# Batch 1's q transposes moved into one group beside its first keys, and half 1's output transposed in two parts

## The chip, the cores and the metric

One core of one Trainium2 chip. The time is the device time of one execution in microseconds (us). Span is what the profiler sees of the same execution; it is 1.7 us less than the time (231.48 against 229.75 us in the profiled run of the kernel before).

## The reference, cut to what matters

```python
# q, k, v: (4 batches, 8 heads, 768 rows, 64); 8 blocks of 96 rows
P = sinkhorn(sort_net)                        # 8 x 8 for each batch and head
k_sorted, v_sorted = P @ blocks(k), P @ blocks(v)
attn = softmax(scale * q_block @ k_sorted_block.T) @ v_sorted_block
x = heads_side_by_side(attn)                  # (3072, 512)
h = x @ w_in                                  # 512 -> 2048
out = (s * relu(h) ** 2 + b) @ w_out          # 2048 -> 512
```

## The kernel before

Rows are done in eight halves of a batch (0 to 7, 384 rows each; half 1 is the second half of batch 0, and batch 1 starts with half 2). `ffn1(t)` makes the hidden layer of half t: for each of eight pairs of hidden blocks, eight products `hps` on TensorE (PE), relu `rt` on ScalarE (ACT), the squaring `gt` on VectorE (DVE). `ffn2(t)` makes the output, `ops`. Between their products PE gets other work from a queue: scores `sc`, attention outputs `pv`, sorted keys `tk`, sorted values `tv`, transposes of q (`tq`) and of attention outputs (`tr`). Each of these fills a PSUM tile that ACT or DVE must copy out. GpSimd (POOL) meanwhile sums the rows of w_out (`csum`) for the bias term.

```python
def t_piece(t, eng, n0=0, nn=HB):      # all head pairs: 16 transposes, one copy by eng
    ...
def t_part(t, hp0, eng, n0, nn):       # head pairs hp0, hp0+1: 8 transposes, one copy
    ...
# the place of the change (cut)
ffn1(0, Queue([seq(SC(1, 2), P(1, 0)), V1(0), seq(SC(1, 3), P(1, 1)), P(1, 2), V1(1), P(1, 3),
               seq(V1(2), V1(3)), lambda: t_piece(1, "v")], 8), 2, 2)
V1(4)()                                # V1: sorted values of batch 1, tv -> ACT copy vn -> DRAM
V1(5)()
q_piece(1, 0, "s")                     # 24 transposes of q, one copy by ACT
...
csums(0, 8)                            # POOL, once half 1's attention output is there
v_read(1, nc.sync)                     # the values come back from DRAM as vs
ffn1(1, ...)
...
ffn2(0, qu)                            # qu: q_piece(1, 2), keys of batch 1, bias product, ...
```

A queue of eight pieces gives one after each pair of hidden blocks. In the traces ACT and DVE start what they are given in the order of the program (ACT in before: rt at 43.37 us, two vn from 43.76, rt at 44.70; DVE gt at 45.26, xt at 45.72).

The softmax here doesn't subtract the row's maximum and nothing guards it: scores larger than these inputs give would overflow.

Of the kernel before, what the change touches and what calls it, by code (L numbers as in the profile page):

```python
# [18 lines left out]
def kernel(  # L19
# [22 lines left out]
    HB = NB // 2  # L42
# [51 lines left out]
    def load_k(rows, prow, n=1):  # L94
        for c0 in range(0, BLK, BLK // n):
            cs = slice(c0, c0 + BLK // n)
            nc.gpsimd.dma_start(out=kb[prow, cs, :], in_=kraw[rows, cs, :])
# [4 lines left out]
    def brows(b):  # L102
        return slice(b * 64, (b + 1) * 64), slice((b % 2) * 64, (b % 2) * 64 + 64)
# [132 lines left out]
    def evac(out, in_, eng):  # L236
        if eng == "v":
            nc.vector.tensor_copy(out=out, in_=in_)  # L238
        else:
            nc.scalar.copy(out=out, in_=in_)  # L240
# [20 lines left out]
    def q_piece(b, hp0, eng):  # L261

        if hp0 == 0:
            QT[b] = qtp.tile([128, NHP, S], BF, tag="qt", name=f"qt{b}")
        ps = psa.tile([128, 2, 1024], BF, tag="a", name="tq")
        for i in range(2):
            for t in range(TQ):
                for e in range(2):
                    nc.tensor.transpose(
                        out=ps[e * 64:(e + 1) * 64, i, t * 128:(t + 1) * 128],  # L270
                        in_=qr[b][:, 2 * (hp0 + i) + e, t, :], identity=ident)
        evac(QT[b][:, hp0:hp0 + 2, :].rearrange("q a (p t) -> q a p t", t=TQ),
             ps[:, :, 0:S].rearrange("q a (t p) -> q a p t", t=TQ), eng)
# [55 lines left out]
    def v_piece1(c0, eng):  # L329

        pr = brows(1)[1]
        ps = psb.tile([128, 8, D], FP, tag="b", name="tv")
        lhsT = pd1[pr].rearrange("p e m i -> p (e m i)")
        hb = BLK // 2
        for hf in range(2):
            nc.tensor.matmul(out=ps[hf * 64:(hf + 1) * 64], lhsT=lhsT,
                             rhs=vb[pr, hf * hb + c0:hf * hb + c0 + 8, :],
                             start=True, stop=True)
        vn = vnp.tile([128, 16, D], BF, tag="vn", name="vn")
        evac(vn[:, 0:8, :], ps, eng)  # L340
        for hf in range(2):
            nc.sync.dma_start(out=dv[1][:, hf * hb + c0:hf * hb + c0 + 8, :],
                              in_=vn[hf * 64:(hf + 1) * 64, 0:8, :])

    def v_piece2(c0, eng):

        ps = psa.tile([128, 16, D], FP, tag="a", name="tv")
        lhsT = pd2.rearrange("p b e m i -> p (b e m i)")
        for i in range(2):
            nc.tensor.matmul(out=ps[:, i * 8:(i + 1) * 8, :], lhsT=lhsT,  # L350
                             rhs=vb[:, c0 + i * 8:c0 + i * 8 + 8, :], start=True, stop=True)
        vn = vnp.tile([128, 16, D], BF, tag="vn", name="vn")
        evac(vn, ps, eng)
        nc.sync.dma_start(out=dv[2][:, c0:c0 + 16, :], in_=vn)
# [81 lines left out]
    def t_piece(t, eng, n0=0, nn=HB):  # L436

        x = X[t]
        if t not in XT:
            XT[t] = xtp.tile([128, NHP, TG], BF, tag="xt", name="xt")  # L440
        if nn < HB:
            t1 = psb.tile([128, 1024], BF, tag="b", name="tr")
            tr = [t1[:, hp * nn * BLK:(hp + 1) * nn * BLK] for hp in range(NHP)]
            src = t1[:, 0:NHP * nn * BLK]
            dst = XT[t][:, :, n0 * BLK:(n0 + nn) * BLK]
            src = src.rearrange("p (a t) -> p a t", a=NHP)
        else:
            t2 = psa.tile([128, 2, 1024], BF, tag="a", name="tr")
            tr = [t2[:, hp // 2, (hp % 2) * TG:(hp % 2 + 1) * TG] for hp in range(NHP)]
            src = t2[:, :, 0:2 * TG]  # L450
            dst = XT[t].rearrange("p (a b) t -> p a (b t)", b=2)
        for hp in range(NHP):
            for n in range(n0, n0 + nn):
                nc.tensor.transpose(out=tr[hp][:, (n - n0) * BLK:(n - n0 + 1) * BLK],
                                    in_=x[:, n, hp * 128:(hp + 1) * 128],
                                    identity=ident[0:BLK, 0:BLK])
        evac(dst, src, eng)

    def t_part(t, hp0, eng, n0, nn):

        if t not in XT:
            XT[t] = xtp.tile([128, NHP, TG], BF, tag="xt", name="xt")
        tr = psa.tile([128, 2, 1024], BF, tag="a", name="tr")
        for i in range(2):
            hp = hp0 + i
            for n in range(n0, n0 + nn):
                nc.tensor.transpose(out=tr[:, 0, (i * nn + n - n0) * BLK:(i * nn + n - n0 + 1) * BLK],
                                    in_=X[t][:, n, hp * 128:(hp + 1) * 128],
                                    identity=ident[0:BLK, 0:BLK])
        evac(XT[t][:, hp0:hp0 + 2, n0 * BLK:(n0 + nn) * BLK],  # L470
             tr[:, 0, 0:2 * nn * BLK].rearrange("p (a t) -> p a t", a=2), eng)
# [16 lines left out]
    def ffn1(t, slot=nothing, n0=0, nn=HB, lead=0):  # L488
        if t not in GT:
            GT[t] = gtp.tile([128, NF, TG], BF, tag="gt", name="gt")  # L490
        gt = GT[t]
        c0, nt = n0 * BLK, nn * BLK
        begun = {}

        def products(f0, hps, part):
            for f in range(2):
                for hp in part:
                    nc.tensor.matmul(out=hps[:, f, 0:nt], lhsT=wi_at(hp, f0 + f),  # L498
                                     rhs=xt_at(t, hp, n0, nn),
                                     start=(hp == 0), stop=(hp == NHP - 1))  # L500

        for f0 in range(0, lead, 2):
            begun[f0] = psa.tile([128, 2, 512], FP, tag="a", name="hps")
            products(f0, begun[f0], range(0, NHP // 2))
        for f0 in range(0, NF, 2):
            if f0 in begun:
                hps = begun[f0]
                products(f0, hps, range(NHP // 2, NHP))
            else:
                hps = psa.tile([128, 2, 512], FP, tag="a", name="hps")  # L510
                products(f0, hps, range(NHP))
            rt = rtp.tile([128, 2, TG], BF, tag="rt", name="rt")
            nc.scalar.activation(out=rt[:, :, 0:nt], in_=hps[:, :, 0:nt], func=AF.Relu)  # L513
            nc.vector.tensor_tensor(out=gt[:, f0:f0 + 2, c0:c0 + nt], in0=rt[:, :, 0:nt],  # L514
                                    in1=rt[:, :, 0:nt], op=ALU.mult)
            slot()
# [59 lines left out]
    def seq(*fs):  # L576
        def run():
            for f in fs:
                f()
        return run  # L580

    def S2(t, hp):
        return lambda: (s_piece(t, hp), s_piece(t, hp + 1))

    def P2(t, hp):
        return lambda: (p_piece(t, hp), p_piece(t, hp + 1))

    def T(t):
        return lambda: x_turn(t)

    def attn(t):
        return [S2(t, 0), nothing, P2(t, 0), S2(t, 2), nothing, P2(t, 2), nothing, T(t)]
# [54 lines left out]
    def P(t, hp, *r):  # L647
        return lambda: p_piece(t, hp, *r)

    def SC(t, hp):  # L650
        return lambda: s_piece(t, hp)

    def V1(i, eng="s"):
        return lambda: v_piece1(i * 8, eng)
# [1 line left out]
    ffn1(0, Queue([P(0, 0, 2, 2), P(0, 1, 2, 2), P(0, 2, 2, 2), P(0, 3, 2, 2),  # L656
                   lambda: q_half(1, "s"), lambda: t_piece(0, "v", 2, 2), SC(1, 0), SC(1, 1)], 8), 0, 2, 2)
    ffn1(0, Queue([seq(SC(1, 2), P(1, 0)), V1(0), seq(SC(1, 3), P(1, 1)), P(1, 2), V1(1), P(1, 3),
                   seq(V1(2), V1(3)), lambda: t_piece(1, "v")], 8), 2, 2)
    V1(4)()  # L660
    V1(5)()
    q_piece(1, 0, "s")


    csum = const.tile([128, d_model], FP)
# [16 lines left out]
    def K(b, c0, nc2, eng):  # L682
        return lambda: k_piece(b, c0, nc2, 1, eng)()

    V2 = [lambda c0=c0: v_piece2(c0, "s") for c0 in range(0, BLK, 16)]
    qu = Queue([nothing, seq(lambda: q_piece(1, 2, "s"), K(1, 0, 16, "v")), nothing,
                seq(K(1, 32, 16, "s"), K(1, 64, 16, "v")), nothing,
                seq(lambda: load_k(*brows(2)), lambda: load_q(2), bias_piece),
                V2[0], S2(2, 0), V2[1], S2(2, 2), V2[2], V2[3], P2(2, 0), V2[4], P2(2, 2), V2[5],
                seq(T(2), S2(3, 0), K(2, 0, 16, "s")), P2(3, 0), nothing,  # L690
# [13 lines left out]
    qu = Queue([S2(4, 0), nothing, nothing, P2(4, 0), nothing, S2(4, 2), nothing, nothing,  # L704
                P2(4, 2), nothing, T(4), nothing, seq(S2(5, 0), K(3, 0, 16, "v")), nothing, nothing,
                P2(5, 0), nothing, seq(S2(5, 2), K(3, 32, 16, "s")), nothing, P2(5, 2),
                K(3, 64, 16, "s"), T(5),
                lambda: q_turn(3), nothing], 24)
# [4 lines left out]
    qu = Queue(attn(6) + attn(7), 24)  # L713
# [36 lines left out]
```

## Time and profile before

| | |
|---|---|
| time, median of 4 runs | 231.46 us (230.92 to 231.69) |
| PE busy | 97% of the span |
| from the pv at 75.62 us to the end | 154.13 us, PE without a gap to its last product, which ends at 226.42 us |

Two more lines of the page of the kernel before, the busy times and the granted PE clock in tenths, one digit for each 5.7 us:

```profile
PE 223.2 (97%) x2034; PEld 136.3 (59%) x2034; DVE 116.0 (50%) x244; ACT 115.7 (50%) x165; POOL 48.1 (21%) x62
...
PEclk9995699999999999999999999999999999999999
```

With PE busy 97%, what is to be won or lost by moving work is idle PE time, a few tenths of a microsecond at a time. The digits 5 and 6 are a stretch at half clock (0.50 granted) near 17 to 27 us.

### The profile page before, as it was taken

The numbers are of one execution on the slowest core, as the hardware profiler recorded it, in microseconds if no ns is written. First come the engines' busy times: TensorE is split into PE (matmuls) and PEld (weight loads), VectorE is DVE, ScalarE is ACT, GpSimd is POOL, SyncE is SP. The second block draws the span as 40 slices with busy tenths as digits, with TensorE's granted clock in tenths as the row PEclk, the third lists the DMA queues.
The fourth block names the chain that finished last, engine by engine and source line by source line (L and its number), as shares of the span: only waits on it lengthen the run. The fifth ranks groups of instructions, "written<-read, shape, count | busy, mean of one in ns | idle before, by whom it ended". The sixth has DMA issues, their size and how long they took to land.

```text
span 229.8 us, 4833 instructions
## 1 busy us (share of the span) xinstructions
PE 223.2 (97%) x2034; PEld 136.3 (59%) x2034; DVE 116.0 (50%) x244; ACT 115.7 (50%) x165; POOL 48.1 (21%) x62
## 2 busy tenths in 40 slices
PE   8979999999999999999999999999999999999994
PEld 5879888765554565665555555655555556654442
DVE  4778666638991554344345843434443634441221
ACT  5268479685358387866621285565322245660000
POOL 7920000299992000008730000000000000000000
PEclk9995699999999999999999999999999999999999
DMA  5899999999399998645999996610115250001212
GB/s 93 137 199 214 223 195 205 227 219 203 70 122 180 314 247 136 126 116 70 133 142 150 183 176 134 76 47 0 49 46 121 87 114 0 3 0 46 86 54 91
DMA packets 46694, 28.90 MB, mean 126 GB/s; under 512 B 35920, under 2 KB 41040, under 8 KB 46160
## 3 DMA queue, kind: packets, MB, share of 16 engines
q0 software_dynamic: 18800, 15.21, 46.5%
q1 hardware_dynamic: 27728, 13.32, 26.8%
q8 instruction: 16, 0.26, 0.5%
q10 hardware_dynamic: 144, 0.07, 0.1%
q14 instruction: 6, 0.05, 0.1%
HBM read 29.63 MB, written 8.65 MB: 167 GB/s over the span
## 4 chain that ended last, share of the span: by engine, by line
PE 80%; DMA 14%; ACT 3%; DVE 1%; issue 0%; SPq 0%
PE hps L498 31%; PE ops L552 30%; DMA dv<-vn 8%; DMA vs<-dv 6%; PE wp L182 6%; PE pv L402 4%; PE sc L375 3%; PE tv L320 2%; PE ops L537 2%; PE tk L294 1%; ACT ks L240 1%; PE tq L254 1%; ACT qt L240 1%; PE tv L350 0%; ACT rt L513 0%
## 5 line engine op out<-in xcount | busy, mean ns | idle before, releaser
L498 PE MATMUL hps<-xt,wi 128*128 128x384 bf16 (+1 forms) x576 | 87.0, 308 | 0.2
L552 PE MATMUL ops<-wo,gt 128*128 128x512 bf16 x368 | 85.8, 379 | 0.0
L498 PEld LDWEIGHTS <-wi 128*128 128x128 bf16 x576 | 53.7, 98 | 30.6 <-issue 1.1
L513 ACT ACTIVATE rt<-hps 128x768 bf16<-128x768 f32 (+1 forms) x72 | 53.1, 740 | 37.0 <-PE hps L498 36.1
L514 DVE TENSOR_TENSOR gt<-rt 128x768 bf16<-128x768 bf16 (+1 forms) x72 | 41.6, 580 | 49.5 <-ACT rt L513 49.3
L552 PEld LDWEIGHTS <-gt 128*128 128x128 bf16 x368 | 34.0, 98 | 37.9 <-issue 0.6
L378 ACT ACTIVATE at<-sc 96x768 bf16<-96x768 f32 x32 | 24.4, 803 | 30.2 <-PE sc L375 30.1
L526 DVE SCALAR_TENSOR_TENSOR ot<-ops,s_bc,bias 128x512 f32<-128x512 f32 x23 | 17.2, 750 | 40.4 <-PE ops L552 40.3
L407 DVE TENSOR_TENSOR x<-pv,rec 96x512 bf16<-96x512 f32 (+1 forms) x36 | 22.6, 628 | 1.3
L240 ACT CAST ks<-tk 64x512 bf16<-64x512 f32 (+1 forms) x32 | 18.6, 582 | 4.2 <-PE tk L294 3.9
L674 POOL TENSOR_TENSOR csum<-csum,wo 128x512 f32<-128x512 f32 x14 | 17.6, 1254 | 1.0
L182 PE MATMUL wp<-zt 128*128 128x256 bf16 x84 | 13.5, 329 | 1.1 <-DVE warm L113 1.1
L402 PEld LDWEIGHTS <-at 96*128 96x128 bf16 (+1 forms) x256 | 12.0, 104 | 4.3 <-DMA vs<-dv 0.8
L238 DVE CAST ks<-tk 64x512 bf16<-64x512 f32 (+1 forms) x20 | 13.1, 654 | 2.1 <-PE tk L294 1.8
L402 PE MATMUL pv<-vs,at 96*128 96x66 bf16 (+1 forms) x256 | 13.0, 199 | 0.4 <-DMA vs<-dv 0.3
L240 ACT CAST vn<-tv 128x512 bf16<-128x512 f32 (+1 forms) x12 | 9.4, 800 | 6.8 <-DMA out_dram<-ot 3.8
L84 POOL DMA_DIRECT2D qr<-in_q_dram x12 | 10.6, 913 | 5.3 <-DMA kb<-in_k_dram 2.9
L375 PEld LDWEIGHTS <-ks 64*96 64x96 bf16 x256 | 8.3, 128 | 5.7 <-issue 4.3
L406 DVE RECIPROCAL rec<-pv 96x8 f32<-96x8 f32 (+1 forms) x36 | 6.9, 193 | 9.1 <-PE pv L402 9.1
L182 PEld LDWEIGHTS <-zt 128*128 128x128 bf16 x84 | 9.5, 117 | 3.2 <-DVE warm L113 1.1
L375 PE MATMUL sc<-qt,ks 64*96 64x96 bf16 x256 | 10.7, 219 | 0.0
L240 ACT COPY qt<-tq 128x768 bf16<-128x768 bf16 (+1 forms) x6 | 5.9, 1014 | 5.0 <-PE tq L254 3.3
(72 smaller groups left out, 97.5 us busy)
## 6 DMA issues: line engine op xcount, KB each, us to landing
out_dram<-ot SPq DMA_DIRECT2D x23, 256.0 KB, 2.8
kb<-in_k_dram POOLq DMA_DIRECT2D x4, 768.0 KB, 11.1
vb<-in_v_dram POOLq DMA_DIRECT2D x4, 768.0 KB, 18.9
wi<-in_moe_w_in_dram POOLq DMA_DIRECT2D x2, 1024.0 KB, 19.6
wo<-in_moe_w_out_dram POOLq DMA_DIRECT2D x2, 1024.0 KB, 32.5
qr<-in_q_dram POOLq DMA_DIRECT2D x12, 128.0 KB, 17.7
dv<-vn SPq DMA_DIRECT2D x6, 256.0 KB, 6.6
vs<-dv POOLq DMA_DIRECT2D x4, 384.0 KB, 13.1
```

What stands on the lines that cost most here:

```text
L182: nc.tensor.matmul(out=wp, lhsT=zt[:, 0:128], rhs=zt, start=True, stop=True)
L240: nc.scalar.copy(out=out, in_=in_)
L375: nc.tensor.matmul(out=sc[:, e, n * BLK:(n + 1) * BLK], lhsT=ks[pr, g0 + n, :], rhs=QT[b][pr, hp, q0:q0 + BLK], start=True, stop=True)
L378: nc.scalar.activation(out=at, in_=sc[:, :, 0:TG], func=AF.Exp, scale=scale)
L402: nc.tensor.matmul(out=pv[e][0:m, (n - n0) * VW:(n - n0 + 1) * VW], lhsT=atf[:, c0:c0 + m], rhs=VS[b][:, gi, :], start=True, stop=True)
L407: nc.vector.tensor_tensor(out=x[:, n0:n0 + nn, hp * 128:(hp + 1) * 128].rearrange("p n (e d) -> p e n d", e=2), in0=pvv[:, :, :, 0:D], in1 ...
L498: nc.tensor.matmul(out=hps[:, f, 0:nt], lhsT=wi_at(hp, f0 + f), rhs=xt_at(t, hp, n0, nn), start=(hp == 0), stop=(hp == NHP - 1))
L513: nc.scalar.activation(out=rt[:, :, 0:nt], in_=hps[:, :, 0:nt], func=AF.Relu)
L514: nc.vector.tensor_tensor(out=gt[:, f0:f0 + 2, c0:c0 + nt], in0=rt[:, :, 0:nt], in1=rt[:, :, 0:nt], op=ALU.mult)
L526: nc.vector.scalar_tensor_tensor(out=ot, in0=ops, scalar=s_bc, in1=bias, op0=ALU.mult, op1=ALU.add)
L552: nc.tensor.matmul(out=ops, lhsT=gt[:, f, m * 128:(m + 1) * 128], rhs=wo_at(f), start=(f == 0), stop=(f == NF - 1))
L674: nc.gpsimd.tensor_tensor(out=csum, in0=csum, in1=wo_at(f), op=ALU.add)
```

## The change

Intent, as the change has it: transposing half 1's output in two parts lets two engines copy it, so that ffn1 of half 1 need not wait for one long copy; the q transposes that filled that wait then stand with the other q transposes and the first keys. The engines of the last copies are balanced anew.

```diff
-                   seq(V1(2), V1(3)), lambda: t_piece(1, "v")], 8), 2, 2)
+                   seq(lambda: t_part(1, 0, "s", 0, HB), V1(2), V1(3)),
+                   lambda: t_part(1, 2, "v", 0, HB)], 8), 2, 2)
     V1(4)()
     V1(5)()
-    q_piece(1, 0, "s")
...
-    qu = Queue([nothing, seq(lambda: q_piece(1, 2, "s"), K(1, 0, 16, "v")), nothing,
-                seq(K(1, 32, 16, "s"), K(1, 64, 16, "v")), nothing,
+    qu = Queue([nothing, seq(lambda: q_piece(1, 0, "s"), lambda: q_piece(1, 2, "v"), K(1, 0, 16, "v")), nothing,
+                seq(K(1, 32, 16, "s"), K(1, 64, 16, "s")), nothing,
```

("s" is ACT, "v" is DVE.)

## The prediction

> **What bounds the kernel now.** I read the page first: TensorE (PE) is busy 97% of the span, VectorE (DVE), ScalarE (ACT) and GpSimd (POOL) 50%, 50% and 21%. PE is the bound, but a share says nothing about a place, so next the chain of waits, in shares and then in order of time. These lines are the shares, and then the stretch up to the first attention output of half 2 (pv at 75.62):
>
> ```profile
> PE 80%; DMA 14%; ACT 3%; DVE 1%; issue 0%; SPq 0%
> ```
>
> ```profile
> 42.82 11.82 DMA dv<-vn
> ...
> 54.66 7.50 DMA dv<-vn
> ...
> 62.69 12.89 DMA vs<-dv
> 75.58 0.05 issue
> 75.62 0.71 PE pv L402 x16
> ```
>
> The chain does not run through PE from 42.8 to 75.6 us. It runs through the sorted values of batch 1: PE makes them (tv), ACT copies them (vn), they go to DRAM and come back as vs, and PE's pv at 75.62 needs them. After 75.62 the chain is PE alone to the end. So whatever the change does between 42.8 and 75.6 us counts only by when PE gets to that pv, and not before 75.58 us. The timeline there:
>
> ```profile
> 74.34 1.03 PE L552 MATMUL ops<-wo,gt 128*128 128x512 bf16 x4
> ...
> 75.62 0.71 PE L402 MATMUL pv<-vs,at 96*128 96x66 bf16 x16 [0.26 <-DMA vs<-dv]
> ```
>
> Four ops matmuls start every 0.216 us (their step in the trace), so PE was free at 74.34 + 4 x 0.216 = 75.20 us and waited to 75.62: 0.42 us. (The 0.26 that the line prints counts from a modelled end.) That is the whole slack on this path. Third, the timeline where the edited code lies, the end of ffn1 of half 0 and the start of ffn1 of half 1:
>
> ```profile
> 43.37 0.49 ACT L513 ACTIVATE rt<-hps 128x384 bf16<-128x384 f32 x1 [0.44 <-PE hps L498]
> ...
> 43.76 1.07 ACT L240 CAST vn<-tv 128x512 bf16<-128x512 f32 x2
> ...
> 44.43 1.14 POOL L672 TENSOR_TENSOR csum<-wo 128x512 f32<-128x512 bf16 x1
> 44.49 0.85 PE L454 MATMUL tr<-ident,x 96*128 96x96 bf16 x16
> 44.70 0.52 ACT L513 ACTIVATE rt<-hps 128x384 bf16<-128x384 f32 x1
> 45.26 0.53 DVE L514 TENSOR_TENSOR gt<-rt 128x384 bf16<-128x384 bf16 x1 [0.83 <-ACT rt L513]
> ...
> 45.65 1.16 POOL L674 TENSOR_TENSOR csum<-csum,wo 128x512 f32<-128x512 f32 x1
> ...
> 45.72 0.94 DVE L238 COPY xt<-tr 128x1536 bf16<-128x1536 bf16 x1
> 45.81 0.70 PEld L269 LDWEIGHTS <-qr 128*64 128x64 bf16 x24 [0.41 <-issue]
> ...
> 46.71 0.11 PEld L498 LDWEIGHTS <-wi 128*128 128x128 bf16 x2 [0.20 <-DVE xt L238]
> ```
>
> Half 1's output is transposed by 16 matmuls at 44.49, copied by one DVE copy at 45.72 that ends at 46.66, and its first product starts at 46.72. In between PE does four tv and the 24 q transposes (tq) from 45.81. A second group like it takes 0.79 us at 59.41 where nothing is waited for; here it holds PE 0.90 us, so PE really waits 0.1 us. The filler fits the copy almost exactly: there is next to nothing to win here.
>
> [...] DVE's squarings gt, and GpSimd's weight sums beside them:
>
> ```profile
> 49.07 0.62 DVE L514 TENSOR_TENSOR gt<-rt 128x768 bf16<-128x768 bf16 x1 [2.41 <-ACT rt L513]
> 50.37 0.75 DVE L514 TENSOR_TENSOR gt<-rt 128x768 bf16<-128x768 bf16 x1 [0.68 <-ACT rt L513]
> ```
>
> ```profile
> 48.12 1.16 POOL L674 TENSOR_TENSOR csum<-csum,wo 128x512 f32<-128x512 f32 x1
> ```
>
> ```profile
> 49.35 1.35 POOL L674 TENSOR_TENSOR csum<-csum,wo 128x512 f32<-128x512 f32 x1
> ```
>
> The sums end at 49.28 and 50.70, the gt at 49.69 and 51.12: each gt ends 0.41 us after a sum, whenever it was ready. For the half-size gt at 45.26 it is 45.79 - 45.57 = 0.22 us. The copies from PSUM (xt) run beside a sum undisturbed: 0.94 us within the sum of 45.65 to 46.81.
> [...] ACT's rt and vn above run one after the other as the program has them.
> [...] In this trace the last ops before a q or key group (59.41, 62.61) holds PE 0.31 us and not 0.216: 0.09 us for a change.
>
> **The change part by part.**
> (1) The q group of heads 0 to 3 leaves the place before ffn1 of half 1 and stands in ffn2 of half 0, in front of the other one and of the first keys. The number of PE instructions stays (4061 rows either way in the built program). Added there: 24 transposes at 28 ns = 0.67 us, without a change of mode of their own. Removed here: 0.90 us, of which 0.79 is work and mode changes.
> (2) Half 1's transposes come in two parts. The first eight stand after the seventh pair of hidden blocks, in front of two tv pairs, and ACT copies them; the other eight stay at the end, and DVE copies them. I lay this out, with durations from the trace (steps from start to start: ACT rt to next 0.39, vn 0.47, a 128x768 copy 0.69 as the earlier qt copies have, a DVE copy of 128x768 0.55 long):
> - PE: products from 42.51 as before, first eight transposes 43.18 to 43.62, two tv pairs to 44.17, last products to 44.84, second eight to 45.28, two tv pairs to about 45.86. The waits of the built program (PSUM banks freed by rt at 43.86 and by x at 44.16) are met in time.
> - ACT: rt 43.37, xt first half 43.76, vn 44.45, vn 44.92, and only then the last rt, at 45.39 to 45.91. Before it ran at 44.70: 0.69 us later, the length of the new copy.
> - DVE: the last gt could start at 45.95. In the old run it got in behind the first sum (end 45.57). Now the second sum, 45.65 to 46.81,[...]: gt ends at 46.81 + 0.22 = 47.02. The second xt copy stands behind it in order: 46.95 to 47.50.
> - PE: ffn1 of half 1 starts at 45.86, does two matmuls (0.33 us: head pairs 0 and 1, in the half that ACT copied) and waits for head pair 2 until about 47.54. It then stands as if it had started at 47.54 - 0.33 = 47.21, and before it was 46.72: **+0.49 us**, in spite of the q group being gone. A hole of 1.35 us opens where 0.1 was.
> (3) The second q copy goes from ACT to DVE, and one key piece (four casts of about 0.6 us) from DVE to ACT. ACT has idle time there (2.1 us before 67.74) and DVE's queue gets lighter by four casts of 0.69 less one copy[...]. The first score piece needs all keys: ACT ends them at about 69.1, PE is there at about 69.7. No cost.
> Sum until that pv: +0.49 + 0.67 = +1.16 us, so PE comes at 75.20 + 1.16 = 76.36. The values land at about 75.6 as before: the chain to them goes through the second vn at 41.73, ahead of the edit, and the last writes of dv wait for the earlier ones to land (issued 54.66), not for vn. So the old 0.42 us wait vanishes, and the rest stays: 76.36 - 75.62 = **+0.74 us**. After it PE has no gap to absorb it. 231.67 + 0.74 = 232.4 us.
>
> **The rivals.**
> (A) The intent comes true: the two halves are copied side by side on two engines and ffn1 of half 1 starts at 45.86, 0.86 us earlier. Then the q group added later takes 0.67 of it, PE is at the pv 0.19 us earlier, and the DMA holds it there anyway: 231.7. For it: two engines, half the copy each. Against: ACT's and DVE's order, both read from the built program.
> (B) The last gt slips in between two sums. Then gt ends at about 46.3, xt at 46.8, ffn1 as if from 46.5: -0.2 + 0.67 = +0.47, less the 0.42: 231.7 to 231.8. For it: the sums leave gaps of 0.08 us. Against: each later gt waited for one to end.
> (C) In ffn2 of half 0 DVE is late: gt there take 1.5 us each and are behind until 61.2, perhaps 62.6 now; then the strided q copy and four casts end at 65.5 to 67, and the bias product, which takes their PSUM bank, is due at 66.5. Up to +0.6: 233.0.
> (D) The dv writes of the two delayed vn (0.7 us) push vs back by as much. To cost, vs would have to land after 76.36; only beyond that it adds. [...] Against: the last issues wait for other writes.
>
> **Range and chances.** (2) as laid out gives 232.4, A and B 231.7, C and D up to 233.0. The three runs before span 0.44 us, so noise is about 0.2. I weigh my layout at six in ten: 232.3 with 231.6 to 233.0. Two per cent are 4.6 us; no rival comes near. [...]
>
> **What would show it.** Right: the last half-size rt at about 45.4, gt ending 0.2 us after a sum, xt ending near 47.5, two hps matmuls and then an idle PE of over 1 us for DVE's xt; 48 tq in a row at about 60 us lasting some 1.45 us; no wait for vs at the pv, which starts at 76.2 to 76.5. Wrong: ffn1 of half 1 going on before 46.7 without a hole, a wait for vs that remains, or a new wait for a PSUM bank at the bias product.

The marked cuts are statements that no trace here shows. That the last gt ends 0.22 us after the second sum is an estimate from the squarings shown (each ends 0.41 us after a sum, the half-size one 0.22). "A change" is one of tile in the trace, from the `128*128` of ops to the `128*64` of tq or the `64*128` of tk. That a sum leaves the copies alone shows in the smaller xt copy, 0.55 us beside a sum (47.06 in after) and 0.55 without one (34.47 in before).

## The result, and the profile after

232.82 us, median of 4 runs (232.77 to 232.94), against 231.46 us: 1.36 us slower. The ratio is 1.0063 (95% interval 1.0043 to 1.0083). A ratio is the mean time of one kernel's runs over that of the other's runs of the same rounds, so it isn't quite the ratio of the medians. Executions over 1.5% slower than the fastest of the same kernel are left out of the means. Within 2% it is the same; the interval says that it is slower.

The chain of waits of the changed kernel, first in shares and then in order of time (start, length, what):

```profile
PE 84%; DVE 10%; ACT 3%; issue 1%
```

```profile
46.08 1.06 DVE gt L514
47.14 0.48 DVE xt L238
47.66 1.15 PE hps L498 x6
...
49.68 7.33 DVE gt L514 x5
...
62.45 1.74 DVE qt L238
...
66.21 0.71 DVE ks L238
67.05 1.10 PE bps L596 x2
```

The DMA share of 14% is gone, and DVE has 10%: from 46 to 67 us the chain runs through DVE's squarings and copies up to the bias product bps. Two places are to be looked at. First the boundary in the timeline (start, length, engine, line, operation, what it writes and reads, count; in brackets the idle time before it and what ended that):

```profile
43.88 0.79 ACT L240 COPY xt<-tr 128x768 bf16<-128x768 bf16 x1
...
44.56 1.09 ACT L240 CAST vn<-tv 128x512 bf16<-128x512 f32 x2
...
45.51 0.53 ACT L513 ACTIVATE rt<-hps 128x384 bf16<-128x384 f32 x1
...
46.04 0.50 PE L498 MATMUL hps<-xt,wi 128*128 128x384 bf16 x2
46.08 1.06 DVE L514 TENSOR_TENSOR gt<-rt 128x384 bf16<-128x384 bf16 x1 [1.54 <-ACT rt L513]
47.06 0.55 DVE L238 COPY xt<-tr 128x768 bf16<-128x768 bf16 x1
47.66 2.11 PE L498 MATMUL hps<-xt,wi 128*128 128x384 bf16 x12 [1.12 <-DVE xt L238]
```

ACT copies its half first, then two vn, and only then the last small rt. DVE's gt starts at 46.08, takes 1.06 us where it took 0.53, and the other half is copied after it. PE does two hps and stands. The two matmuls around the hole start 1.45 us apart, and 0.163 apart elsewhere: a hole of 1.29 us.

Second the bias product: the kernel before, then PE and DVE of the changed kernel at the same place:

```profile
61.10 5.63 DVE L238 CAST ks<-tk 64x512 bf16<-64x512 f32 x8
...
65.38 1.02 PE L596 MATMUL bps<-csum,onesf 128*128 128x512 f32 x2
```

```profile
64.92 1.90 PE L552 MATMUL ops<-wo,gt 128*128 128x512 bf16 x8
67.05 1.10 PE L596 MATMUL bps<-csum,onesf 128*128 128x512 f32 x2 [0.23 <-DVE ks L238]
```

```profile
59.59 2.94 DVE L514 TENSOR_TENSOR gt<-rt 128x768 bf16<-128x768 bf16 x2
62.45 1.74 DVE L238 COPY qt<-tq 128x1536 bf16<-128x1536 bf16 x1
64.12 2.79 DVE L238 CAST ks<-tk 64x512 bf16<-64x512 f32 x4
```

The bias product writes the PSUM bank that DVE's first four key casts free. In before they ended at 63.88, well ahead of it. Here they end at 66.90; PE was there at 64.92 + 8 x 0.217 = 66.66 us. From the last ops to bps it is 0.604 us instead of 0.216, and the second bps comes 0.504 us after the first instead of 0.430: 0.46 us lost.

**An account that does not depend on the execution.** Let A be the start of the last hps group but one of half 0 (42.51 us in the kernel before), the last point ahead of all edits. In all executions A lies between 42.46 and 43.25 us. In the kernels that keep the pieces after it in order, the first pv of half 2 (75.62 in the first profile of before) is followed by 154.12 to 154.13 us, up to one execution with 154.19. So what the edits do stands in "pv minus A" alone. Before: 33.115 us, of which 0.425 is the wait for the values, so 32.69 of work. After: 34.313, without a wait. The difference of 1.62 us is: ffn1 of half 1 starts at A + 3.41 instead of A + 4.21 but has a hole of 1.29 (+0.49), the joint q group (1.463 us long against 0.794, +0.67), and the bias product (+0.46). They add to 1.62.

### The profile page after: what moved, and what is told of

It is laid out like the page before. It is cut to its first block, busy times and chain, and to the rows that moved or that the text cites. A ratio compares the mean times of both kernels' runs of the same rounds, so it can differ in the third digit from the quotient of the medians.

```text
span 231.1 us, 4815 instructions
## 1 busy us (share of the span) xinstructions
PE 222.3 (96%) x2014; PEld 136.6 (59%) x2034; DVE 117.7 (51%) x241; ACT 117.3 (51%) x169; POOL 48.2 (21%) x62
## 4 chain that ended last, share of the span: by engine, by line
PE 84%; DVE 10%; ACT 3%; issue 1%
PE ops L552 32%; PE hps L498 32%; DVE gt L514 6%; PE wp L182 6%; PE pv L402 4%; PE sc L375 3%; PE tv L320 2%; PE ops L537 2%; PE tk L294 1%; ACT ks L240 1%; DVE ks L238 1%; PE tv L350 1%; ACT rt L513 1%; PE tq L254 1%; DVE qt L238 1%
## 5 line engine op out<-in xcount | busy, mean ns | idle before, releaser
L552 PE MATMUL ops<-wo,gt 128*128 128x512 bf16 x348 | 82.9, 379 | 1.3 <-issue 0.3
L514 DVE TENSOR_TENSOR gt<-rt 128x768 bf16<-128x768 bf16 (+1 forms) x72 | 44.9, 630 | 47.9 <-ACT rt L513 47.7
L240 ACT CAST ks<-tk 64x512 bf16<-64x512 f32 (+1 forms) x36 | 20.9, 581 | 4.9 <-PE tk L294 4.5
L238 DVE CAST ks<-tk 64x512 bf16<-64x512 f32 (+1 forms) x16 | 10.3, 645 | 2.0 <-PE tk L294 1.8
L320 PE MATMUL tv<-pd,vb 64*128 64x64 bf16 x64 | 6.2, 267 | 1.4 <-issue 1.1
```

The costliest lines, as they stand in the source:

```text
L240: nc.scalar.copy(out=out, in_=in_)
L514: nc.vector.tensor_tensor(out=gt[:, f0:f0 + 2, c0:c0 + nt], in0=rt[:, :, 0:nt], in1=rt[:, :, 0:nt], op=ALU.mult)
L552: nc.tensor.matmul(out=ops, lhsT=gt[:, f, m * 128:(m + 1) * 128], rhs=wo_at(f), start=(f == 0), stop=(f == NF - 1))
```

## The experiments

Twelve kernels ran, two of them (b1, a2) repeats; all results were correct. The numbers "pv minus A" are from each profile; times are medians. Runs were sent in groups that shared the runs of before.

| run | time, us | before, us | ratio (95%) | pv minus A, us |
|---|---|---|---|---|
| changed kernel | 232.82 | 231.46 | 1.0063 (1.0043 to 1.0083) | 34.31 |
| e1 q and engines alone | 231.97 | 231.23 | 1.0034 (1.0019 to 1.0050) | 33.34 |
| e2 split alone | 231.97 | 231.23 | 1.0030 (1.0014 to 1.0046) | 33.28 |
| e3 sums later | 232.13 | 231.23 | 1.0033 (1.0018 to 1.0047) | 33.52 |
| e4 engines back | 232.26 | 231.23 | 1.0044 (1.0030 to 1.0058) | 33.85 |
| b1 before again | 231.03 (one run, state unknown) | 231.40 | | 32.69 |
| e5 both copies on DVE | 231.83 | 231.40 | 1.0023 (1.0006 to 1.0039) | 33.20 |
| e6 a values piece first | 231.29 | 231.40 | 0.9999 (0.9984 to 1.0015) | 33.99, with 1.30 of other work |
| e7 q groups early | 231.95 | 231.40 | 1.0023 (1.0008 to 1.0037) | 33.30 |
| a2 changed again | 232.84 (one run, state unknown) | 231.20 | | 34.44, 0.13 of it a wait for values |
| e8 q early, copied by ACT | 231.72 | 231.20 | 1.0022 (1.0009 to 1.0034) | 33.28 |
| e9 both mendings | 231.22 | 231.20 | 1.0001 (0.9988 to 1.0015) | 32.74 |
| e10 q early, values piece first | 231.87 | 231.20 | 1.0029 (1.0016 to 1.0043) | 35.18, with 1.30 of other work |

### e1: the moved q group and the new engines, without the split

```diff
 # against the changed kernel
-                   seq(lambda: t_part(1, 0, "s", 0, HB), V1(2), V1(3)),
-                   lambda: t_part(1, 2, "v", 0, HB)], 8), 2, 2)
+                   seq(V1(2), V1(3)), lambda: t_piece(1, "v")], 8), 2, 2)
```

> Part 1 and 3 alone: the first q group of batch 1 stands in ffn2 of half 0, the second is copied by VectorE and the last keys by ScalarE, but half 1's output is transposed in one piece as before. My theory: the loss of the whole change is a sum, 0.50 (hole before ffn1 of half 1) + 0.67 (q group moved) + 0.46 (wait of the bias product for its bank) - 0.42 (slack before the values of batch 1 arrive). Here ffn1 of half 1 starts when it did (46.7, PE idle some 0.85 us before it, since the xt copy still ends at 46.66), so PE is 0.67 us late; VectorE is less late than in the whole change, and the bias product, due at 66.05, finds its bank free at about 65.6: no wait. PE at the first pv of half 2 at 75.87 against 75.62: +0.25 us against before. Rival 1, moving the q group is the whole loss: +1.2 to 1.4. Rival 2, the split is the whole loss: 0.

0.74 us slower than before in the medians. The account agrees with the sum (pv minus A is 0.65 over before's 32.69, 0.67 expected; the bias product waits for nothing), but PE never waited for the values, so nothing was taken off: the 0.25 us failed by its slack term.

### e2: the split alone

```diff
 # against the kernel before
-                   seq(V1(2), V1(3)), lambda: t_piece(1, "v")], 8), 2, 2)
+                   seq(lambda: t_part(1, 0, "s", 0, HB), V1(2), V1(3)),
+                   lambda: t_part(1, 2, "v", 0, HB)], 8), 2, 2)
```

> Part 2 alone: half 1's output transposed in two parts, first copied by ScalarE; the q groups, their copies and the keys as before. My theory: the last gt is held by the second weight sum on GpSimd, xt ends near 47.5, so PE stands 0.5 us behind; the q group is in the hole, at 45.9 to 46.8, and the hole that is left is some 0.4 to 0.5 us. The slack of 0.42 takes nearly all of it: +0.07 us against before, no wait for vs left. Rival, the split itself is the whole loss: +1.2 us or more. Rival, the split gains and only the moved q loses: below -0.2 us.

0.74 us slower in the medians, not 0.07. Again the parts are as expected: gt takes 1.06 us, a hole of 0.50 us is left behind the q group, and pv minus A is 0.59 over before (0.50 of it the hole, 0.12 a score piece that waits, less 0.02 in small differences). Again there was no slack: the values landed at 70.6 us and PE came at 75.81. The rival "the split gains and only the moved q loses" falls.

### e3: GpSimd's second sum after the copy

```diff
 # against the changed kernel
-    csums(0, 8)
+    csums(0, 2)
+    nc.gpsimd.tensor_copy(out=gate, in_=XT[1][0:1, NHP - 1, TG - 1:TG])
+    csums(2, 8)
```

> The whole change, but GpSimd's second weight sum waits (a one-element copy that reads the last element of half 1's transposed output) until the second xt copy is done; seven of the sums stand as they were in order, about 1.2 us later. My theory[...]: the last half-size gt takes 0.35 us and not 1.06, xt ends at about 46.9, the hole shrinks from 1.35 to about 0.65 us, PE is 0.7 us earlier there; the sums end 1.2 us later, about when the bias product is due, so up to 0.5 us can be given back there. 231.9 to 232.5 against 232.8 of the change. Rival, the hole is ScalarE's order alone: gt keeps its 1.06 us, the hole its 1.35 us.

```profile
46.34 0.36 DVE L514 TENSOR_TENSOR gt<-rt 128x384 bf16<-128x384 bf16 x1 [1.54 <-ACT rt L513]
...
47.22 1.30 PE L498 MATMUL hps<-xt,wi 128*128 128x384 bf16 x7 [0.42 <-DVE xt L238]
```

The last gt took 0.36 us instead of 1.06, the hole shrank from 1.29 to 0.58 us, and 0.38 us were lost at the bias product, which now had to wait for the sums. Pv minus A fell by 0.79, 232.13 us is in the range. The length of gt, and with it 0.70 us of the hole, came from GpSimd's second sum beside it; by what means the sum holds gt up is not shown.

### e4: the engines of the last copies as before

```diff
 # against the changed kernel
-lambda: q_piece(1, 2, "v"), K(1, 0, 16, "v")), nothing,
-                seq(K(1, 32, 16, "s"), K(1, 64, 16, "s")), nothing,
+lambda: q_piece(1, 2, "s"), K(1, 0, 16, "v")), nothing,
+                seq(K(1, 32, 16, "s"), K(1, 64, 16, "v")), nothing,
```

> The whole change, but the second q copy on ScalarE and the last keys on VectorE as before. My theory: VectorE goes from its last gt of ffn1 of half 1 (ends 62.5) straight to the first keys, which end at about 65.2; the bias product, due at 66.7, starts without a wait (last ops to bias 0.216 us and not 0.604). 0.46 us faster than the change: +0.9 us or somewhat less against before. Rival, bias waits for the weight sums and not for the bank: no gain, the wait stays.

The timeline of PE at the bias product:

```profile
64.81 1.90 PE L552 MATMUL ops<-wo,gt 128*128 128x512 bf16 x8
66.55 1.02 PE L596 MATMUL bps<-csum,onesf 128*128 128x512 f32 x2
```

No wait; pv minus A fell by exactly the 0.46 us. Rival C of the prediction is thereby what happened, by the q copy's place on DVE: the edit moves the last keys back too, but they stand behind the casts that free the bank, so they can't have held them. (One of its five runs took 237.44 us, a slow one, and is left out of the ratio.)

### b1 and a2: the two kernels once more, for a second profile

> The kernel before, unchanged, for a second profile of it. The runs of parts alone came out 0.75 and 0.70 us over before where I expected 0.25 and 0.07, and in their traces PE never waits for the values of batch 1, which landed between 70.6 and 76.0 us. So the 0.42 us that I took as slack was a wait of one execution. New theory: from the seventh pair of hidden blocks of half 0 (the last products of it but one; start A) to the first pv of half 2 PE needs 32.69 us in before, and waits for the values only in some executions; after that pv 154.13 us are left in every kernel. This profile: pv at A + 32.7, with no wait or a short one. Old theory: a wait of 0.3 to 0.5 us again, pv near 75.6.

The same place of before in this execution:

```profile
74.34 1.03 PE L552 MATMUL ops<-wo,gt 128*128 128x512 bf16 x4
75.20 0.70 PE L402 MATMUL pv<-vs,at 96*128 96x66 bf16 x16
```

A is the same as in the first profile (42.51), and pv comes at 75.20, where I had said that PE is free, without a wait. The span is 229.32 against 229.75 us: the 0.43 us were one execution's. The values came at 70.8 us here and at 75.6 in the first profile. Over all profiles they came between 69.7 and 77.6.

> The changed kernel, unchanged, for a second profile. From the start of the seventh product pair (A) to the first pv of half 2: 34.31 us as in the first profile, in the same three terms (hole 1.29, joint q group 1.46 long, bias product 0.46 late), if they are the kernel's and not one execution's; 154.13 us after the pv. If a term is chance, as the wait for the values was, it is missing here.

The three terms are there again (1.445 us between the two matmuls of the hole; 0.603 and 0.504 us at the bias product). Pv minus A is 34.44, but in this execution the values landed at 76.9 us and PE waited 0.13 us for them; without that it is 34.31.

### e5: both halves of the transposed output copied by DVE

```diff
 # against the changed kernel
-                   seq(lambda: t_part(1, 0, "s", 0, HB), V1(2), V1(3)),
+                   seq(lambda: t_part(1, 0, "v", 0, HB), V1(2), V1(3)),
```

> The whole change, but the first half of the transposed output is copied by VectorE too, so ScalarE has no copy in front of its last half-size rt. My theory (ScalarE's order makes gt late[...]): rt about 0.4 us earlier than in the change, so that gt is queued at 45.65 on the change's clock, before the first weight sum ends at 45.69[...]; xt ends at 46.4, the hole shrinks from 1.29 us to about 0.1, and PE is 0.5 to 1.2 us earlier at the pv (A + 33.1 to 33.8 instead of 34.31). The margin is 0.04 us: where gt misses it, the hole stays at about 1.3. Rival, the hole is VectorE's copy itself: the hole stays or grows, with gt early.

The last rt, gt and copy, and the sums beside them (A is 0.14 us later here than in the changed kernel's profile):

```profile
44.69 1.14 POOL L672 TENSOR_TENSOR csum<-wo 128x512 f32<-128x512 bf16 x1
...
45.29 0.49 ACT L513 ACTIVATE rt<-hps 128x384 bf16<-128x384 f32 x1
...
45.81 0.36 DVE L514 TENSOR_TENSOR gt<-rt 128x384 bf16<-128x384 bf16 x1 [0.66 <-ACT rt L513]
45.91 1.27 POOL L674 TENSOR_TENSOR csum<-csum,wo 128x512 f32<-128x512 f32 x1
```

With ACT's copy gone, gt starts as the first sum ends (45.83) and takes 0.36 us; the second sum, which starts beside it at 45.91, is the one that is longer (1.27 instead of 1.16 us). The hole is 0.28 us (I had said about 0.1), pv minus A 33.20, the 1.11 us less lie in the range that I gave. So the order of ACT's queue made gt miss its turn, and in the changed kernel it ended 0.21 us after the sum that ran then: 0.70 us of its 1.06 are the miss. The rival falls.

### e9: both mendings

```diff
 # against the changed kernel: e5's edit and e4's edit together
-                   seq(lambda: t_part(1, 0, "s", 0, HB), V1(2), V1(3)),
+                   seq(lambda: t_part(1, 0, "v", 0, HB), V1(2), V1(3)),
...
-lambda: q_piece(1, 2, "v"), K(1, 0, 16, "v")), nothing,
+lambda: q_piece(1, 2, "s"), K(1, 0, 16, "v")), nothing,
-                seq(K(1, 32, 16, "s"), K(1, 64, 16, "s")), nothing,
+                seq(K(1, 32, 16, "s"), K(1, 64, 16, "v")), nothing,
```

> The whole change with both mendings: both halves of the transposed output copied by VectorE, the second q copy on ScalarE and the last keys on VectorE. If the terms add, PE is at the pv at A + 33.20 - 0.46 = 32.74, as in before (32.69), and the time is before's within 0.1 us: moving the q group alone costs nothing, only the waits that it and the copies make. Rival, a wait is left that neither mending takes: 33.0 or more.

Pv minus A is 32.741 (expected 32.74) and the time is before's: 231.22 against 231.20 us. The two terms of waiting are all of the loss. The moved q group adds its 0.67 us where it now stands and takes as much from where it stood, if nothing else waits.

### e6: is there a steady wait for the values to be won?

```diff
 # against the kernel before
-V2[2], V2[3], P2(2, 0), V2[4], P2(2, 2), V2[5],
+V2[2], V2[3], V2[4], P2(2, 0), P2(2, 2), V2[5],
```

> The kernel before, with the fifth values piece of batches 2 and 3 in front of the first pv of half 2 instead of behind it, so that PE has 0.43 us of other work plus four ops there while it waits for the values of batch 1. Old theory (a steady wait of 0.42 us): 0.4 us faster than before. New theory (a wait in some executions only, about 0.1 us in the mean): 0 to 0.15 us faster, not told from nothing by five rounds, but no run with a wait for vs.

Nothing (ratio 0.9999), as the new theory has it. The interval can't show 0.1 us; the 0.4 us of the old theory, a ratio of 0.9983, lies just outside it.

### e7, e8, e10: the change turned round

```diff
 # e7 against the kernel before; e8: q_piece(1, 2, "s"); e10: e8 and e6 together
     q_piece(1, 0, "s")
+    q_piece(1, 2, "v")
...
-seq(lambda: q_piece(1, 2, "s"), K(1, 0, 16, "v"))
+K(1, 0, 16, "v")
```

> The change turned round: the kernel before, with the second q group moved up to the first, before ffn1 of half 1, and copied by VectorE; the transposes in one piece, the keys as before. My theory counts PE time alone: the 0.1 us wait before ffn1 of half 1 is filled, the joint group saves one change of mode (0.12 us), and no engine is late: PE at the pv at A + 32.45 to 32.5 instead of 32.69, 0.2 us faster than before if the values are there. Rival, the joint group keeps two PSUM banks and the copies of 1.4 to 1.7 us hold up the first products or the first rt of half 1: a new wait, slower than before by 0.3 or more.

> As the turned-round change (both q groups before ffn1 of half 1, transposes in one piece), but the second q copy on ScalarE, where it was before. In the first form VectorE's copy of 1.76 us[...], all squarings after it came late, and the bias product and the score piece waited 0.20 and 0.48 us. My theory: without it VectorE runs as in before and ScalarE has the time; PE at the pv at A + 32.45 to 32.55 against 32.69, so 0.15 to 0.25 us faster in every execution without a wait for the values. Rival, ScalarE's two copies in a row (2.9 us) hold up the first rt of half 1 and by it the third PSUM bank: A + 33 or more.

> The kernel of q groups early (ScalarE copies) and the fifth values piece in front of the first pv of half 2. If the first is 0.2 us faster, this is too, and has in addition no execution that waits for the values of batch 1 (0.43 us in one of the two profiles of before): 0.2 to 0.35 us faster than before in the mean. PE at the pv at A + 33.75 to 33.85 and 152.84 us after it.

All three are slower than before, and none of my expectations held. The boundary did what I wanted (in e7 and e8 ffn1 of half 1 starts behind the joint group without a hole). But ffn1 of half 1 starts 0.56 us later after A, its squarings start later, and as I read the traces some lose their turn to a sum. DVE of e8:

```profile
58.00 4.36 DVE L514 TENSOR_TENSOR gt<-rt 128x768 bf16<-128x768 bf16 x3
62.28 5.63 DVE L238 CAST ks<-tk 64x512 bf16<-64x512 f32 x8
67.94 0.75 DVE L597 TENSOR_SCALAR bias<-bps,b_bc 128x512 f32<-128x512 f32 x1
```

In before these squarings started at 56.81, the casts at 61.10 and the bias at 66.76. DVE is 1.2 us later, and the bias product and the score piece behind it wait 0.19 and 0.64 us (in e7 0.21 and 0.65; the 0.48 in the expectation of e8 was misread). In e7 I blamed DVE's q copy for that. That was wrong: e7's own trace has the copy end at 49.51, before the rt of the first squaring ends at 49.96, and e8, without the copy, has the same delay. What e7 and e8 share is a late first squaring (49.99 in e7; 50.19 in e8, with ACT's two q copies in front of its rt; 49.07 in before). Both engines then run against each other without a pause, a squaring every 1.43 us, while PE makes one due every 1.30, and what DVE is behind at the start it is behind at the end. That the late first squaring is the cause, and an earlier one would have kept its turn, I argue from the traces; no run tries it. In e10 the values landed at 77.6 us, and PE waited 0.60 us for them, even with the piece in front.

## Why the prediction was right or wrong, point by point

The time, 232.82 us, lies in the range (231.6 to 233.0), within 2% as given. The predicted loss was about 0.7 us, the measured 1.36, so the sum was too small by half, by two terms that erred the same way. That the time still lies in the range is owed to the room given to rivals C and D, not to the sum.

- **Part 1, right.** The joint group took 1.463 us (said: 1.45); the addition is 0.67.
- **Part 2, right.** On a clock that is 0.12 us later (A is), the last rt came at 45.51 (said: 45.39), gt ended 0.21 us after the second sum (said: 0.22), xt ended at 47.61 (47.50), and after two matmuls ffn1 stood until 47.66 (47.54). A hole of 1.29 us (1.35) and +0.49 us. Rival A falls with it, and rival B did not occur.
- **Part 3 failed: "No cost."** I had DVE's queue lighter and the bias product safe, with rival C at up to 0.6 us. It cost 0.46. DVE's q copy took 1.74 us, and the last squaring ended at 62.53, at the late end of rival C. The q copy reads PSUM in steps of 128 elements; it took 1.74 us where the xt copy of the same size and a unit step took 0.94, both on DVE. That the step is the cause no run tries apart, and the trace of before has no such copy on DVE that I could have taken the time from.
- **The slack failed: "the old 0.42 us wait vanishes, and the rest stays".** I took one execution's wait for the values for a property of the kernel. In b1 it was 0; the values land anywhere in 8 us, and in nine of the 14 profiles (of all kernels) before 75.2 us, when PE was free in before. Where there was nothing to vanish, the whole of the three terms stays: a2's span is 1.82 us over b1's, of which 1.62 are the three terms, 0.13 the wait for the values in a2 and 0.07 the time after the pv. The 1.36 us of the medians are less, and the record shows one reason. All five runs of the changed kernel had a granted clock of 0.977 or 0.978. Of the 29 runs of before whose clock is listed, 15 had 0.969 or 0.970 and took 231.47 us in the mean; the seven at 0.978 took 231.01. At the same clock the loss is about 1.8 us (232.84 less 231.01); the medians compare unlike executions.
- **After the pv, right.** No gap absorbs anything: 154.13 us in both kernels.
- **Rival D** did not occur: in the first profile after, the values landed at 75.53 us, as before at 75.58. But a2 had them at 76.9, late enough to cost 0.13, in a kernel that is no different. No run tells the two delayed vn from the usual spread there.

## What to carry to other kernels

A copy given to an idle engine isn't free. Here the last rt stood behind the added copy in ACT's order and came 0.69 us later after A (45.51 against 44.70 us, with A 0.12 later), and the squaring that needs it met a running GpSimd sum (1.16 us) and took 1.06 us, where it took 0.36 in e3 without that sum beside it. Count the loss where the last copy is waited for, not by busy shares. And before a wait that ends with a DMA is booked as slack, profile the same kernel twice: PE's work from A to the pv repeated to 0.01 us here, the landing of a transfer only to some us. Where the loss looked for is under 1%, compare executions of the same granted clock too.

## What else the traces show

- A 128x768 squaring (0.56 us alone) and a 128x512 sum (1.16 us alone), both busy, alternate here, one of each every 1.43 us, and each squaring ends 0.41 us after a sum.
- From the last of a run of ops to the first matmul of a q, key or score group (tiles `128*64`, `64*128` and `64*96` after `128*128`) it was 0.31 us instead of 0.216. To a pv (`96*128`) it stayed at 0.216 (b1, four ops from 74.34 to 75.20).
- PE was at half clock (0.50) for 10.24 us in before, to 26.88 us, though busy 8.68 of 9.10 us between 16.7 and 25.8 us, by the profile's modelled ends. In the changed kernel's first profile it was so to 27.23 us; in e1 it still was from 27 to 29 us, where before had 1.00. A moved with it, 42.51, 42.63 and 43.25 us: it is a source of the spread between executions. What keeps the clock low there was not tried.
- The landing of one and the same transfer spreads: 69.7 to 77.6 us for the last read of batch 1's values, over 14 profiles. Its issue moved too, from 56.9 to 62.8 us, and from issue to landing it took 8.9 to 15.3 us.
